# Layer 1 of the tails in seven products, all steady z by DMA transposes, and a reordered head

## The chip, the cores and the metric

The kernel runs on one core of a Trainium2 chip. The metric is the device time of one execution in microseconds (us); lower is better. A core has TensorE (matmuls, into the eight PSUM banks), VectorE (DVE), ScalarE (ACT), GpSimd (POOL) and SyncE (SP), which here only issues DMAs. Each engine runs its instructions in the order of the program and waits for others by semaphores.

## What is computed

Windowed causal attention over 8 images of 8 heads, 576 positions and 64 features, then a normalised two-layer perceptron with a residual. Cut to what matters:

```
scores = (q @ k.T) / 8          # keys i-63 .. i only
attn   = exp(scores) / sum      # per row
x      = attn @ v               # heads side by side: 512 features
z      = (x - mean) / sqrt(var + 1e-6)
out    = x + relu((z * g) @ W1) @ W2    # W1: 512 x 2048, W2: 2048 x 512
```

## The kernel before

**Tiling.** The work is cut into nine groups of 512 tokens: the first 512 positions of each of the eight images (groups 0 to 7), and the 64 last positions of all eight ("tails", group 8). A group has four blocks of 128 tokens. For a block, `s_mm` makes the scores on TensorE and their exponentials on ScalarE, `s_mask` masks them on VectorE, `b_step` multiplies with v on TensorE and then normalises and takes the statistics on VectorE, `r_step` makes the reciprocal deviation on ScalarE, `z_step` makes z on VectorE, and z is transposed into `zT`, features on partitions, which layer 1 reads. There are two ways for that: `zt_step` (lines 447 to 458), four TensorE transposes into a PSUM tile "tp" and a copy by ScalarE, and `x_step` (lines 460 to 464), one DMA transpose issued by SyncE.

**The order.** The order is written out by hand. Period g runs the perceptron of group g as a list of units, and after each unit a slot of steps for the attention of group g+1, placed by `at(unit, step, ...)`. A steady period (g = 2 to 7) has 16 layer 1 units `l1(hc)`, each four matmuls of 512 columns evacuated by a ScalarE relu into `hrT` (lines 508 to 516), and 14 layer 2 units. Layer 2 uses a seven-product scheme: `presum` makes sums of quarters of `hrT` on VectorE (`sw`), `t_weights` sums of quarters of W2 (`tw`), `product(n, t)` (lines 573 to 596) runs eight matmuls of 256 columns, and `post` (lines 600 to 618) adds a finished product to the output on VectorE, which frees its PSUM bank ("X", "Y" or "Z"). In period 7 the attention of group 8 runs beside. Period 8 has only the perceptron of the tails.

**Steady attention.** For groups 3 to 7, `steps` (lines 781 to 793) places block bj: `b_step` at unit ub (4, 8, 12, 17), `r_step` and `z_step` two and two or three units later, then `x_step` at ub+3 for blocks 0 to 2; block 3 goes by `zt_step` at unit 23. In the same period SyncE issues the loads of the next image but one (`load_qk`, `load_v`), and `x_main` (lines 277 to 286), two DMA transposes for each half of q and k after ScalarE's casts `cast_q`, at units 17 and 19. The first scores of an image follow after unit 0 of the next period. Group 2 is prepared in period 1 with `zt_step` for all four blocks; group 8 in period 7 with `zt_step` at units 3, 7, 12 and 17 (the table `TAILS`, lines 751 to 761).

**The head.** Before period 0 (lines 667 to 724) image 0 is loaded and cast, GpSimd casts q and k (`cast_q`) and v, `t_main` transposes q and k on TensorE, `vB_cur` and `vB_prev` make a copy of v that is shifted by half a block. `w1_cast(i, c, engine, lo, hi)` scales and casts a 512-column piece of W1, piece i = 2*quarter + half of the rows, row chunk c. `keep_clock(n)` runs n matmuls whose result is not used. Casts of image 1, of W2 and later loads are in `rest_of_loads` (lines 731 to 746).

**Buffers.** Pool tags are shared: "pt" (six) for the exponentials, "qk32_x" and "qk16_x" (two each) for loaded and cast q and k, PSUM tags "sc" (2), "xps" (1, two banks), "tp" (2), "mm" (2). `pace(t)` copies one column on GpSimd so that its queue waits for t.

Of the kernel before, what the change touches and what calls it, by code (L numbers as in the profile page):

```python
# [18 lines left out]
def kernel(  # L19
# [129 lines left out]
    def cast_q(b, x, half, act=False):  # L149
        t = qk32.pop((b, x, half))  # L150
        dst = p_in.tile([128, 8, 2, D], FP16, tag=f"qk16_{x}", name=f"qk16_{x}_{b}_{half}")
        qk16[(b, x, half)] = dst
        j = 8 if b < NPE else 2 if x == 1 else 4
        cp(act, dst[:, :].rearrange("p (a j) e d -> p a e j d", j=j),
           t[:, :].rearrange("p (a e j d) -> p a e j d", e=2, j=j, d=D))

    def alloc_v(b):
        vA[b] = p_va.tile([128, 4, H, D + 1], FP16, tag="vA", name=f"vA_{b}")
        nc.gpsimd.memset(vA[b][:, :, :, D:D + 1], 1.0)
# [18 lines left out]
    def cast_v(b, c0, c1, act=False):  # L178
        cp(act, vA[b][:, c0:c1, :, 0:D], v32[b][:, c0:c1])
# [72 lines left out]
    def alloc_qkT(b):  # L252
        qkT[b] = [p_qkt.tile([128, NHP, SM + 64 * x], FP16, tag=f"qkT{x}", name=f"qkT{x}_{b}") for x in range(2)]
        if b >= NPE:
            nc.gpsimd.memset(k_runs(b)[:, :, 0:32], 0.0)
        else:
            nc.gpsimd.memset(qkT[b][1][:, :, 0:64], 0.0)
# [4 lines left out]
    def evac(x, out, in_):  # L262
        if x == 0:
            nc.scalar.copy(out=out, in_=in_)
        else:
            nc.vector.tensor_copy(out=out, in_=in_)

# [98 lines left out]
        ptv = pt[:, :].rearrange("p a h w i -> p (a h w) i")  # L366
        nc.vector.tensor_tensor(out=ptv, in0=ptv, in1=mb, op=ALU.mult)  # L367

    def b_step(g, kb):
        kblk = f"{g}_{kb}"  # L370
        if kb % 2 == 0:
            x_norm[(g, kb // 2)] = p_xn.tile([128, 2, H, D], FP32, tag="xn", name=f"xn_{kblk}")
        xn = x_norm[(g, kb // 2)][:, kb % 2]
        xps = ps_x.tile([128, H, 128], FP32, tag="xps", name=f"xps_{kblk}")
        pt = pts.pop((g, kb))
        for h in (0, 2, 4, 6, 1, 3, 5, 7):
            par, hp = h % 2, h // 2
            for r in range(2):
                if g == NGRP - 1:
                    rhs = vt8[:, kb, r, h, :]  # L380
                else:
                    rhs = (vA if r else vB)[g][:, kb, h, :]
                nc.tensor.matmul(out=xps[64 * r:64 * r + 64, h, :D + 1], lhsT=pt[:, par, hp, r, :], rhs=rhs,  # L383
                                 start=True, stop=True)
        rcp = p_blk.tile([128, H], FP32, tag="rcp", name=f"rcp_{kblk}")
        rcps[(g, kb)] = rcp
        nc.vector.reciprocal(out=rcp, in_=xps[:, :, D])
        rcp_b = bass.AP(tensor=rcp.tensor, offset=rcp[:, :].offset,
                        ap=[rcp[:, :].ap[0], rcp[:, :].ap[1], [0, D]])
        nc.vector.tensor_tensor(out=xn, in0=xps[:, :, 0:D], in1=rcp_b, op=ALU.mult)  # L390
        stats = p_blk.tile([128, nc.vector.BN_STATS_DIM], FP32, tag="stats", name=f"stats_{kblk}")
        nc.vector.bn_stats(out=stats, in_=xn.rearrange("p h d -> p (h d)"))  # L392
        mv = p_blk.tile([128, 2], FP32, tag="mv", name=f"mv_{kblk}", bufs=5)
        nc.vector.bn_aggr(out=mv, in_=stats)
        mvs[(g, kb)] = mv
# [97 lines left out]
    def presum(g, i, c):  # L493
        hr = hrTs[g]
        A = [[hr[:, 8 * d + 4 * c:8 * d + 4 * c + 4, 256 * a:256 * a + 256] for d in range(2)] for a in range(2)]
        if c == 0:
            sw[i] = p_hrt.tile([128, 8, 256], FP16, tag=f"sw{i}", name=f"sw{i}_{g}")
        S = {n: t[:, 4 * c:4 * c + 4] for n, t in sw.items()}
        a, b, op = {1: (A[1][0], A[1][1], ALU.add), 2: (S.get(1), A[0][0], ALU.subtract),
                    3: (A[0][0], A[1][0], ALU.subtract), 4: (A[0][1], S.get(2), ALU.subtract)}[i]  # L500
        nc.vector.tensor_tensor(out=S[i], in0=a, in1=b, op=op)  # L501

    def mlp_units(g, split=0, two=False):
        hrT = p_hrt.tile([128, NHC, 512], FP16, tag="hrT", name=f"hrT_{g}")
# [121 lines left out]
                        units.append(lambda kb=kb, part=part: l2(kb, part))  # L626
        if g == 1:
            return units
        for hc in range(split, NHC):
            units.append(lambda hc=hc: l1(hc))  # L630
        if two:
# [33 lines left out]
    )  # L665
    nc.vector.tensor_scalar(out=mbias, in0=mask, scalar1=-1.0, scalar2=30000.0, op0=ALU.add, op1=ALU.mult)
    alloc_qkT(0)
    cast_q(0, 0, 0)
    alloc_v(0)
    cast_q(0, 1, 0)  # L670
    init_vB(0)
    cast_v(0, 0, 1)
    cast_v(0, 1, 2)
    cast_qk(0, 1)
    cast_v(0, 2, 3)
    cast_v(0, 3, 4)
    w1_cast(0, 0, nc.gpsimd)
    w1_cast(1, 0, nc.gpsimd, 0, 256)
    w1_cast(1, 0, nc.gpsimd, 256, 512)
    for i, lo in ((2, 0), (3, 0), (2, 256)):  # L680
        w1_cast(i, 0, nc.gpsimd, lo, lo + 256)

    for f in (alloc_qkT, alloc_v, init_vB):
        f(1)

    def keep_clock(n, pool=ps_t, tag="tp"):
        warm = pool.tile([128, 512], FP32, tag=tag, name="warm")
# [6 lines left out]
    keep_clock(9, ps_mm, "mm")  # L694
    t_main(0, 0, 0, 0)
    keep_clock(1, ps_mm, "mm")
    t_main(0, 1, 0, 1)
    keep_clock(1, ps_mm, "mm")
    vB_cur(0, 0, 0)
    vB_cur(0, 1, 0)  # L700
    vB_prev(0, 0, 1)
    vB_prev(0, 1, 1)
    s_mm(0, 0, True)
    s_mm(0, 1, True, (ps_mm, "mm"))
# [8 lines left out]
    vB_cur(0, 2, 0)  # L713
    keep_clock(2, ps_mm, "mm")
    s_mm(0, 2, True)
    vB_cur(0, 3, 1)
    vB_prev(0, 2, 1)
    keep_clock(1)
    zt_step(0, 1)
    w1_cast(0, 1, nc.scalar)  # L720
    b_step(0, 2)
    z_step(0, 2)
    w1_cast(1, 1, nc.scalar)
    s_mm(0, 3, True)


    load_qk(1, 0)
    for i in range(4):
        w2_load(i)

    def rest_of_loads():
        cast_qk(1, 0)
        for i in range(8):
            w2_cast(i)
            if i < 4:
                w2_load(i + 4)
        load_v(1, 0, 2)
        cast_v(1, 0, 1)
        cast_v(1, 1, 2)
        load_qk(1, 1)  # L740
        load_v(1, 2, 4)
        cast_qk(1, 1)
        cast_v(1, 2, 3)
        cast_v(1, 3, 4)
        load_qk(2, 0)
        load_qk(2, 1)

    def tail_casts(i, act, *us):
# [7 lines left out]
            *tail_casts(3, True, 22, 27, 27), (23, x_tail, 3), (23, x_prev, 3), (24, b_step, 8, 0),  # L756
            (24, s_mm, 8, 1)),
        7: ((0, s_mask, 8, 1), (0, z_step, 8, 0), (3, s_mask, 8, 2), (1, b_step, 8, 1), (1, s_mm, 8, 2),
            (3, zt_step, 8, 0), (8, s_mask, 8, 3), (6, b_step, 8, 2), (6, s_mm, 8, 3), (7, zt_step, 8, 1),
            (11, b_step, 8, 3), (12, zt_step, 8, 2), (17, zt_step, 8, 3)),  # L760
    }
    for g in range(NGRP):
        units = mlp_units(g, (8, 16)[g] if g < 2 else 0, g == 0)
# [17 lines left out]
        def steps(bg, bj, ub, us, sg, sj):  # L781
            if us is not None:
                score(us, bg, bj)
            late = ub < 15
            at(ub, b_step, bg, bj)
            if sj < 4:
                score(ub, sg, sj)
            at(ub + 2, r_step, bg, bj)
            at(ub + 2 + (not late), z_step, bg, bj)
            if bj < 3:  # L790
                at(ub + 3, x_step, bg, bj)
            else:
                at(23, zt_step, bg, bj)

        b = g + 1
        if g == 0:
            at(0, b_step, 0, 3)
            at(0, z_step, 0, 3)
            at(0, w1_cast, 2, 1, nc.scalar)
            at(0, w1_cast, 3, 1, nc.scalar)  # L800
            at(0, w1_cast, 3, 0, nc.scalar, 256, 512)
            at(1, zt_step, 0, 2)
            at(2, zt_step, 0, 3)
            for j in range(4):
# [24 lines left out]
            at(26, keep_k, 0)  # L829
            at(27, lambda: nc.gpsimd.memset(vt8[:, :, :, :, D:D + 1], 1.0))  # L830
            at(27, keep_v, 0)
            at(28, alloc_qkT, 2)
            at(28, cast_q, 2, 0, 0)
            at(29, cast_q, 2, 1, 0)
            at(29, make_vB_half, 1)
            at(41, lambda: pace(zT[1][:, 0, 0:1]))
            at(41, cast_q, 2, 0, 1)
            at(43, cast_q, 2, 1, 1)
        if g == 1:
# [27 lines left out]
            for j in range(4):  # L867
                at((13, 16, 19, 22)[j], s_mm, 2, j)
                at((14, 17, 20, 23)[j], s_mask, 2, j)
                bz((16, 19, 22, 25)[j], 2, j)  # L870
                at((20, 23, 26, 29)[j], zt_step, 2, j)
        if g > 0:
            if g == 1:
                for u, i, c in ((12, 1, 0), (13, 1, 1), (14, 2, 0), (15, 2, 1)):
                    at(u, t_weights, i, c)
            if g == 2:
                at(9, late_masks, 8)
                for u, i, c in ((2, 3, 0), (3, 3, 1), (8, 4, 0), (24, 4, 1)):
                    at(u, t_weights, i, c)
            for u, i, c in () if g == 1 else (  # L880
                    (5, 3, 0), (9, 3, 1), (13, 1, 0), (13, 2, 0), (16, 1, 1), (16, 2, 1), (20, 4, 0), (22, 4, 1)):
                at(u, presum, g, i, c)
        if g > 1 and b < B:
# [21 lines left out]
        if 0 < g and b + 1 < B:  # L905
# [5 lines left out]
            if g == 1:  # L911
# [7 lines left out]
                at(12, alloc_v, n)  # L919
                at(12, alloc_vB, n)  # L920
                for u, c, j in ((21, 0, 0), (22, 1, 0), (24, 2, 1), (24, 3, 1)):
                    if c < 3:
                        at(u, (lambda j=j: pace(zT[b][:, 0, 128 * j:128 * j + 1])) if c % 2 == 0 else
                           (lambda j=j: pace(rss[(b, j)])))
                    at(u, cast_v, n, c, c + 1)
                at(24, make_vB, n)
                at(26, keep_v, n)
            else:
# [4 lines left out]
                for u, x, half in ((16, 0, 0), (16, 1, 0), (17, 0, 1), (18, 1, 1)):  # L933
                    at(u, cast_q, n, x, half, True)
                at(17, x_main, n, 0)
                at(19, x_main, n, 1)
                for c in range(4):
                    at((18, 20, 20, 21)[c], cast_v, n, c, c + 1, True)
                at(22, make_vB, n)
# [38 lines left out]
```

## Time and profile before

| what | us |
|---|---|
| runs shown: median (lowest, highest) | 303.54 (303.21, 303.9) |
| profiled execution | 304.84 |
| its span on the core | 303.0 |
| TensorE busy | 289.7 |
| VectorE, ScalarE, GpSimd busy | 194.8, 189.9, 108.8 |
| periods: 2, 3, 4, 5, 6 start at | 92.6, 122.4, 152.2, 182.0, 211.7 |
| period 7, then 8, start at | 242.7, 271.7 |
| last TensorE instruction ends | 297.8 |

The span is the time from the first to the last instruction of the program in one profiled execution; the rest of the execution lies around it. All lines of the profile belong to that execution. In a row for a group of instructions the numbers after the bar are busy time in us and the mean of one in ns, then the idle time of the engine before them and what ended it. L512 is line 512 of the kernel. PE is TensorE, PEld its weight loads, SPq SyncE's issues.

### The profile page before, as it was taken

Reading aid. Unit: us, or ns where it says so; the run is one execution under the profiler, and the core shown is the slowest. Engines: PE = TensorE matmul, PEld = TensorE weight load, DVE = VectorE, ACT = ScalarE, POOL = GpSimd, SP = SyncE. Lnnn points to the kernel's source line nnn. Section 1 sums busy time; section 2 is a strip of 40 time slices with the busy share of each in tenths; the row PEclk is TensorE's granted clock in tenths of the full one; section 3 lists DMA queues with packets and bytes.
Section 4 is the critical chain, followed back from the end, with each engine's and each line's share of the span. In section 5 each row is a group of like instructions: output and inputs, shape, how many; then the busy total and the mean of one; then the engine's idle time right before and its main releaser. Section 6 shows DMA issues by size and latency. Waiting matters only on the chain.

```text
span 303.0 us, 7956 instructions
## 1 busy us (share of the span) xinstructions
PE 289.7 (96%) x3259; PEld 187.1 (62%) x3259; DVE 194.8 (64%) x353; ACT 189.9 (63%) x372; POOL 108.8 (36%) x194
## 2 busy tenths in 40 slices
PE   5788999999999999999999999999999999999993
PEld 2456544765854478547855784578457845884582
DVE  0696317457984997389638954895489877641362
ACT  3598733576856894589368937892785978307500
POOL 3778775997786203400440043004171010000000
PEclk9799999999999999999999999999999999999999
DMA  6999799999957969997999899899967930003005
GB/s 186 279 368 386 252 272 276 278 303 279 219 115 209 259 127 168 298 247 128 189 319 228 105 200 322 196 118 204 276 123 153 158 141 0 2 21 117 2 0 138
DMA packets 108371, 58.03 MB, mean 192 GB/s; under 512 B 82240, under 2 KB 98112, under 8 KB 108336
## 3 DMA queue, kind: packets, MB, share of 16 engines
q1 hardware_dynamic: 103696, 45.50, 67.1%
q0 software_dynamic: 3680, 11.52, 12.6%
q10 hardware_dynamic: 960, 0.53, 0.6%
q8 instruction: 25, 0.41, 0.6%
q14 instruction: 10, 0.08, 0.1%
HBM read 36.70 MB, written 9.44 MB: 152 GB/s over the span
## 4 chain that ended last, share of the span: by engine, by line
PE 75%; DMA 11%; SPq 5%; POOL 3%; ACT 2%; DVE 2%; issue 1%; POOLq 0%
PE hps L512 33%; PE wX L590 16%; PE wZ L590 8%; PE wY L590 4%; DMA v<-in_v_dram 4%; PE xps L383 4%; SPq L83 3%; DMA w2s<-in_moe_w_ch_dram 3%; PE sc L326 2%; PE ch L525 2%; DMA vt<-vA 2%; SPq L173 2%; PE hph L549 2%; DMA qk<-in_k_dram 1%; PE ztp L453 1%; PE sc L333 1%
## 5 line engine op out<-in xcount | busy, mean ns | idle before, releaser
L512 PE MATMUL hps<-zT,w1g 128*128 128x512 f16 x480 | 109.7, 379 | 0.0
L516 ACT ACTIVATE hrT<-hps 128x512 f16<-128x512 f32 x120 | 71.3, 596 | 54.0 <-PE hps L512 52.8
L512 PEld LDWEIGHTS <-w1g 128*128 128x128 f16 x480 | 44.8, 98 | 49.5
L590 PEld LDWEIGHTS <-sw 128*128 128x128 f16 x448 | 43.5, 98 | 5.0
L590 PEld LDWEIGHTS <-hrT 128*128 128x128 f16 x336 | 32.4, 98 | 5.4
L367 DVE TENSOR_TENSOR pt<-pt,mask 128x1024 f16<-128x1024 f16 x28 | 20.0, 713 | 20.9 <-ACT pt L347 12.6
L207 POOL DMA_DIRECT2D vB<-vA x10 | 5.1, 518 | 77.9 <-ACT vA L145 77.6
L472 POOL DMA_DIRECT2D out_dram<-osb x20 | 13.2, 660 | 54.4 <-DVE osb L608 50.1
L392 DVE BATCH_NORM_STATS2 stats<-xn 128x6 f32<-128x512 f32 x36 | 25.0, 695 | 1.2
L390 DVE TENSOR_TENSOR xn<-xps,rcp 128x512 f32<-128x512 f32 x36 | 24.9, 691 | 1.2
L347 ACT ACTIVATE pt<-sc 128x512 f16<-128x512 f32 x40 | 23.7, 594 | 2.5 <-PE sc L326 2.5
L501 DVE TENSOR_TENSOR sw<-hrT 128x1024 f16<-128x1024 f16 x28 | 19.0, 678 | 9.7 <-ACT hrT L516 9.7
L549 PE MATMUL hph<-zT,w1g 128*128 128x256 f16 x192 | 23.7, 273 | 0.4 <-POOL w1g L240 0.2
L414 DVE TENSOR_SCALAR z<-xn,mv,rs 128x512 f16<-128x512 f32 x32 | 19.8, 617 | 5.0 <-ACT rs L404 4.5
L608 DVE TENSOR_TENSOR osb<-wX,xn 128x512 f32<-128x512 f32 (+1 forms) x24 | 14.9, 621 | 9.9 <-PE wX L590 9.9
L353 ACT ACTIVATE pt<-sc 128x512 f16<-128x512 f32 x32 | 17.6, 594 | 5.0 <-PE sc L333 4.6
L147 POOL CAST qk<-qk 128x1024 f16<-128x1024 f32 x16 | 17.1, 1076 | 9.0 <-DMA qk<-in_q_dram 6.0
L549 PEld LDWEIGHTS <-w1g 128*128 128x128 f16 x192 | 17.9, 98 | 3.5 <-POOL w1g L240 0.5
L383 PEld LDWEIGHTS <-pt 128*64 128x64 f16 x576 | 12.1, 110 | 12.8 <-issue 8.5
L525 PE MATMUL ch<-w2s,hrT 128*128 128x512 f16 x80 | 19.8, 379 | 0.0
L456 ACT COPY zT<-ztp 128x512 f16<-128x512 f16 x21 | 12.3, 584 | 9.6 <-PE ztp L453 9.5
L554 ACT ACTIVATE hrT<-hph 128x512 f16<-128x512 f32 x24 | 14.2, 598 | 3.4 <-PE hph L549 3.2
(108 smaller groups left out, 439.3 us busy)
## 6 DMA issues: line engine op xcount, KB each, us to landing
w2s<-in_moe_w_ch_dram SPq DMA_DIRECT2D x12, 512.0 KB, 9.4
out_dram<-osb POOLq DMA_DIRECT2D x12, 512.0 KB, 7.0
qk<-in_q_dram SPq DMA_DIRECT2D x10, 512.0 KB, 7.7
qk<-in_k_dram SPq DMA_DIRECT2D x10, 512.0 KB, 9.5
v<-in_v_dram SPq DMA_DIRECT2D x40, 128.0 KB, 5.9
qk<-in_q_dram SPq DMA_DIRECT2D x12, 256.0 KB, 5.0
qk<-in_k_dram SPq DMA_DIRECT2D x12, 256.0 KB, 4.8
v<-in_v_dram SPq DMA_DIRECT2D x12, 256.0 KB, 5.7
```

Source lines behind the costliest of these rows:

```text
L347: nc.scalar.activation(out=pt[:, par].rearrange("k h w (p j) -> k (h w) p j", j=4), in_=sc[:, :].rearrange("k h w (j p) -> k (h w) p j", j=4),
L367: nc.vector.tensor_tensor(out=ptv, in0=ptv, in1=mb, op=ALU.mult)
L383: nc.tensor.matmul(out=xps[64 * r:64 * r + 64, h, :D + 1], lhsT=pt[:, par, hp, r, :], rhs=rhs, start=True, stop=True)
L390: nc.vector.tensor_tensor(out=xn, in0=xps[:, :, 0:D], in1=rcp_b, op=ALU.mult)
L392: nc.vector.bn_stats(out=stats, in_=xn.rearrange("p h d -> p (h d)"))
L414: nc.vector.tensor_scalar(out=z, in0=x, scalar1=mv[:, 0:1], scalar2=rss[(g, kb)][:, 0:1], op0=ALU.subtract, op1=ALU.mult)
L501: nc.vector.tensor_tensor(out=S[i], in0=a, in1=b, op=op)
L512: nc.tensor.matmul(out=hps, lhsT=w1g[:, kc, 128 * hc:128 * (hc + 1)], rhs=zT[g][:, kc, :], start=(kc == KCS[0]), stop=(kc == KCS[-1]),)
L516: nc.scalar.activation(out=hrT[:, hc, :], in_=hps, func=AF.Relu, bias=0.0, scale=1.0)
L525: nc.tensor.matmul(out=ch[kb], lhsT=hrT[:, hc, 128 * kb:128 * (kb + 1)], rhs=w2s[:, hc, :], start=(hc == 0), stop=(hc == NHC - 1),)
L549: nc.tensor.matmul(out=hps[:, e], lhsT=w1g[:, kc, 128 * hc:128 * (hc + 1)], rhs=zT[g][:, kc, 256 * half:256 * half + 256], start=(kc == KC ...
L590: nc.tensor.matmul(out=xyz[bank][t * two_banks][:, t], lhsT=lhsT, rhs=rhs, start=bool(first and (t == 0 or two_banks) and hc == 0), stop=( ...
```

## The change

- `steps` uses `x_step` for all four blocks of groups 3 to 7 (block 3 at unit 20 instead of `zt_step` at 23); the second `x_main` moves from unit 19 to 20. Blocks 0 to 2 of group 2 and all blocks of group 8 use `x_step` too.
- Layer 1 of group 8 becomes seven products. `l1_wsum` makes four sums of quarters of W1 on VectorE in eight instructions, `l1_zsum` four sums of quarters of zT, both in period 7. `l1_seven` runs 28 units of four matmuls of 256 columns. Of the seven results for each r, three are copied by ScalarE into SBUF (`held`), one is a ScalarE relu, three are added to a held one on VectorE and then clamped at zero, by VectorE for product 3 and by GpSimd for products 1 and 7. The first layer 2 product goes in before the last four of these units, and the `presum` slots of group 8 move.
- Head: `cast_k0` casts the first half of k on VectorE instead of GpSimd; period 1's memsets move ahead of the first casts; the copies of v change engines, two going to GpSimd; W1 casts go from ScalarE and GpSimd to VectorE, two of them between the normalisation and the statistics of block 2 (`mid`), others change engine or range; six `keep_clock` matmuls are placed around the scores and blocks 1 and 2, where there was one.
- Order: v of image 1 is loaded and cast before the last four pieces of W2; casts of image 2 and the second half of image 1's shifted v go from units 28 and 29 to 39 of period 0, behind z of block 1; two paces of period 1 change.

```diff
+    def cast_k0():
+        t = qk32.pop((0, 1, 0))
+        dst = p_in.tile([128, 8, 2, D], FP16, tag="qk16_1", name="qk16_1_0_0")
+        qk16[(0, 1, 0)] = dst
+        for e in range(2):
+            nc.vector.tensor_copy(out=dst[:, :, e], in_=t[:, 512 * e:512 * e + 512].rearrange("p (j d) -> p j d", d=D))
...
+    def l1_wsum(i, c):
+        A = [[w1g[:, 2 * kb + c, 1024 * d:1024 * d + 1024] for kb in range(2)] for d in range(2)]
+        if c == 0:
+            s1w[i] = p_in.tile([128, 2, 1024], FP16, tag=f"qk32_{i % 2}", name=f"s1w_{i}")
...
+        nc.vector.tensor_tensor(out=S[i], in0=a, in1=b, op=op)
...
+    def l1_zsum(g, i):
...
+        nc.vector.tensor_tensor(out=T[i], in0=z_block(g, *a), in1=b, op=ALU.subtract)
...
+        def product(r, n):
+            kind = {1: "X", 6: "X", 7: "X", 4: "X", 2: "Y", 5: "Z", 3: "Z"}[n]
+            ps, first = bank(r, kind)
+            for e in range(2):
+                hc = 2 * r + e
+                for c in range(2):
...
+                    nc.tensor.matmul(out=ps[:, e], lhsT=lhsT, rhs=rhs, start=bool(first and e == 0 and c == 0),
+                                     stop=(e == 1 and c == 1), skip_group_check=True)
+            up, down = slice(2 * r, 2 * r + 2), slice(8 + 2 * r, 10 + 2 * r)
+            if n in (2, 5, 6):
+                held[(r, n)] = p_pt.tile([128, 2, 256], FP32, tag="pt", name=f"l1h_{r}_{n}")
+                nc.scalar.copy(out=held[(r, n)], in_=ps)
+            elif n == 4:
+                nc.scalar.activation(out=hrT[:, down, lo], in_=ps, func=AF.Relu, bias=0.0, scale=1.0)
+            else:
+                out, other = {1: (hrT[:, up, lo], 2), 7: (hrT[:, down, hi], 5), 3: (hrT[:, up, hi], 6)}[n]
+                nc.vector.tensor_tensor(out=out, in0=ps, in1=held.pop((r, other)), op=ALU.add)
+                (nc.vector if n == 3 else nc.gpsimd).tensor_scalar(out=out, in0=out, scalar1=0.0, scalar2=None,
+                                                                   op0=ALU.max)
+
+        order = ((0, 2), (0, 1), (1, 2), (1, 1), (0, 5), (0, 6), (2, 2), (1, 6), (1, 5), (0, 7), (2, 1), (1, 7),
+                 (3, 2), (3, 1), (0, 3), (0, 4), (2, 5), (2, 6), (3, 5), (3, 6), (1, 3), (2, 7), (1, 4), (3, 7),
+                 (2, 3), (2, 4), (3, 3), (3, 4))
...
+        if last:
+            units += l1_seven(g, hrT)
+            units.insert(24, lambda: product(1, 0))
+            units.append(lambda: product(1, 1))
...
     alloc_qkT(0)
+    alloc_qkT(1)
+    alloc_v(0)
+    alloc_v(1)
     cast_q(0, 0, 0)
-    alloc_v(0)
-    cast_q(0, 1, 0)
     init_vB(0)
+    init_vB(1)
+    cast_k0()
...
+    vB_prev(0, 2, 2)
+    vB_cur(0, 3, 2)
     w1_cast(0, 0, nc.gpsimd)
-    w1_cast(1, 0, nc.gpsimd, 0, 256)
-    w1_cast(1, 0, nc.gpsimd, 256, 512)
-    for i, lo in ((2, 0), (3, 0), (2, 256)):
-        w1_cast(i, 0, nc.gpsimd, lo, lo + 256)
-
-    for f in (alloc_qkT, alloc_v, init_vB):
-        f(1)
+    for i, c, lo in ((1, 0, 256), (1, 1, 256), (2, 0, 0), (2, 0, 256), (3, 0, 256)):
+        w1_cast(i, c, nc.gpsimd, lo, lo + 256)
...
-    vB_cur(0, 3, 1)
-    vB_prev(0, 2, 1)
-    keep_clock(1)
+    w1_cast(0, 1, nc.vector)
+    keep_clock(2, ps_mm, "mm")
     zt_step(0, 1)
-    w1_cast(0, 1, nc.scalar)
-    b_step(0, 2)
+    keep_clock(2, ps_mm, "mm")
+    b_step(0, 2, lambda: [w1_cast(1, c, nc.vector, 0, 256) for c in range(2)])
     z_step(0, 2)
-    w1_cast(1, 1, nc.scalar)
     s_mm(0, 3, True)
+    keep_clock(2, ps_mm, "mm")
...
-            (3, zt_step, 8, 0), (8, s_mask, 8, 3), (6, b_step, 8, 2), (6, s_mm, 8, 3), (7, zt_step, 8, 1),
-            (11, b_step, 8, 3), (12, zt_step, 8, 2), (17, zt_step, 8, 3)),
+            (1, x_step, 8, 0), (8, s_mask, 8, 3), (6, b_step, 8, 2), (6, s_mm, 8, 3), (4, x_step, 8, 1),
+            (11, b_step, 8, 3), (9, x_step, 8, 2), (14, x_step, 8, 3)),
...
-            if bj < 3:
-                at(ub + 3, x_step, bg, bj)
-            else:
-                at(23, zt_step, bg, bj)
+            at(ub + 3, x_step, bg, bj)
...
-            at(0, w1_cast, 3, 1, nc.scalar)
-            at(0, w1_cast, 3, 0, nc.scalar, 256, 512)
+            at(0, w1_cast, 3, 1, nc.scalar, 0, 256)
+            at(0, w1_cast, 3, 0, nc.scalar, 0, 256)
+            at(0, w1_cast, 3, 1, nc.scalar, 256, 512)
...
+            if g == NGRP - 2:
+                for u, i, c in ((14, 3, 0), (15, 3, 1), (17, 1, 0), (18, 1, 1), (20, 2, 0), (22, 2, 1),
+                                (24, 4, 0), (26, 4, 1)):
+                    at(u, l1_wsum, i, c)
+                for u, i in ((24, 1), (26, 2), (28, 3), (28, 4)):
+                    at(u, l1_zsum, g + 1, i)
...
-                at(19, x_main, n, 1)
+                at(20, x_main, n, 1)
```

## The prediction

> **What bounds the kernel now.** I read the page's busy line first, then the chain of waits, then TensorE's own timeline, then SyncE's queue, then rows of single operations.
>
> ```profile
> PE 289.7 (96%) x3259; PEld 187.1 (62%) x3259; DVE 194.8 (64%) x353; ACT 189.9 (63%) x372; POOL 108.8 (36%) x194
> ...
> 271.74 13.81 PE hps L512 x64
> 285.56 1.75 PE wX L590 x16
> ```
>
> The second and third lines are from the chain of waits (start, length, what). A busy TensorE may still wait inside its busy time, so I divide: 64 matmuls of 512 columns in 13.81 us are 216 ns each, 16 of 256 columns in 1.75 us are 109 ns each. From 79 us to 297.8 us the chain is TensorE alone in these steps with nothing between, so there each TensorE instruction removed is time removed. Starts of successive matmuls show no wait over 0.7 us after 28.5 us. After 297.8 us come one DVE add, the output DMAs and the end, 5.2 us that the change leaves alone.
>
> ```profile
> 259.13 1.91 PE L590 MATMUL wX<-w2s,hrT 128*128 128x256 f16 x16
> 260.88 0.39 PE L453 MATMUL ztp<-ident,z 128*128 128x128 f16 x4
> 261.10 1.15 PE L590 MATMUL wY<-w2s,hrT 128*128 128x256 f16 x9
> ```
>
> The timeline of TensorE: a group of four transposes holds back the next matmul by 261.10-260.88 = 0.22 us.
>
> ```profile
> 23.37 0.94 PE L549 MATMUL hph<-zT,w1g 128*128 128x256 f16 x7 [0.24 <-POOL w1g L240]
> 25.41 0.40 PE L453 MATMUL ztp<-ident,z 128*128 128x128 f16 x4 [1.10 <-DVE z L412]
> ```
>
> The last waits of the head are on a W1 cast and on z of block 3; from 25.6 us TensorE is packed. So the head ends where z(0,3) ends.
>
> ```profile
> 136.97 5.00 SPq L464 DMA_TRANSPOSE zT<-z  x3
> 142.06 1.26 SPq L279 DMA_TRANSPOSE qkT<-qk  x1
> 143.42 1.29 SPq L283 DMA_TRANSPOSE qkT<-qk  x1
> 144.80 1.29 SPq L279 DMA_TRANSPOSE qkT<-qk  x1
> 146.19 1.28 SPq L283 DMA_TRANSPOSE qkT<-qk  x1
> 147.52 1.20 SPq L93 DMA_DIRECT2D qk<-in_q_dram  x1
> ```
>
> SyncE's queue in a steady period: one issue follows the other without a gap, and from the loads at 118.23 us to those at 147.52 us it takes 29.3 us of a 29.8 us period. It is the second resource with next to no slack.
>
> ```profile
> L240 POOL TENSOR_SCALAR w1g<-w1s,g 128x512 f16<-128x512 f32 x1 | 1.8, 1755 | 1.3 <-DMA w1s<-in_moe_w_ch_dram 1.3
> L147 POOL CAST vA<-v 128x512 f16<-128x512 f32 x16 | 10.2, 648 | 1.4 <-DMA v<-in_v_dram 1.3
> L608 DVE TENSOR_TENSOR osb<-wX,xn 128x512 f32<-128x512 f32 x18 | 12.4, 687 | 6.8 <-PE wX L590 6.8
> L501 DVE TENSOR_TENSOR sw<-hrT 128x1024 f16<-128x1024 f16 x28 | 19.0, 678 | 9.7 <-ACT hrT L516 9.7
> ```
>
> Groups by form: what GpSimd and VectorE take for forms near the new ones (the second number after the bar is ns of one).
>
> **What the Trainium skill says.** "GPSIMD Engine Reference", section 4.1, calls one-input elementwise work on GpSimd roughly line-rate. This trace agrees for the cast (648 ns for 512) and not for TENSOR_SCALAR (1755 ns for 512, 980 for 256). "SBUF — State Buffer", "Who interferes with whom", says that VectorE copies and tensor_scalars in a two-port mode exclude GpSimd and the other way round: z(0,3) took 1.58 us beside GpSimd's memsets of period 1's buffers, z(0,2) 0.49 us. "DMA: Bandwidth & Descriptors", "DMA Transpose (X-bar)", has plain DMA transposes on SyncE and ScalarE queues only; here all 39 are on SyncE's, so new ones must fit in there.
>
> **The change part by part**, against the profiled execution (span 303.0, with 1.8 us around it 304.84).
>
> *Transposes.* zt_step leaves TensorE 12 times: block 3 of images 3 to 7 (5), blocks 0 to 2 of image 2 (3), the four tail blocks (4). 12 x 0.22 = -2.7 us. The 12 evacuations of 0.58 us on ScalarE go too, worth nothing, since TensorE doesn't wait for ScalarE there. Each new transpose takes 1.25 us of SyncE's issue and lands 3.0 us after it (median of 15; 5.2 at most). Needs: z(3,3) is ready at 116.0, lands by 119 to 121, and layer 1 reads it at 122.2: covered. Behind it, the second half's x_main (moved to unit 20) now waits for z. In the period of 142 us: z ready 145.8, issue to 147.1, the q half issued 147.2 instead of 144.80, landing 3.3 to 4.5 us later, 150.5 to 151.7; scores read it at 152.96-0.22. Covered by 1 us; the k half is 2.4 us later (issue 148.5), but the first two score blocks don't read its keys: at 123.2 scores ran before the last x_main had landed (123.6). In period 1 the q half goes from 85.0 to 88.0 us, lands about 92, is read at 92.7. Loads of the next image follow 2.2 us later. I take +0.2 us; bounds 0 and, where the queue overflows, the rival below. In the tail period SyncE is idle: nothing.
>
> *Layer 1 of the tails.* 64 x 216 ns = 13.8 us become 28 products x 4 x 109 ns = 12.2 us: -1.6 us. The weight loads (98 ns) still hide. Now evacuation: 16 ScalarE (0.6 us), 12 VectorE adds (0.69), four VectorE and eight GpSimd clamps. ScalarE and VectorE fit in 12 us. The GpSimd clamp is a TENSOR_SCALAR of 512 elements, not shown with 16-bit input. Bounds: 0.5 us (below the cast, the narrower input) and 1.9 us (the slowest L240, 1858). I take 1.75, the same operation. Replayed: first product in at 0.9 us, its partner's copy done at 1.3, add to 2.0, first clamp from 2.2; six clamps back to back end at 2.2+6x1.75 = 12.7. The first layer 2 product (unit 24, start 10.5) reads their last rows at 11.1: it waits 1.6 us. The last two clamps end at 16.2, and the presums of VectorE queued behind them make a later product about 0.4 us late. +2.0 us at 1.75; nothing below about 1.5; +3.2 at 1.9. Layer 1 alone would then give back its gain.
>
> *Sums for it in period 7.* Eight l1_wsum (0.68) and four l1_zsum (estimate 0.35, half the elements) put 6.8 us on VectorE, which is busy 19.3 of 29.0 us there; 12 of the 13.9 us after unit 14 would be filled in-order ahead of the adds that free PSUM banks. With 0.61 us from start to start, as two independent ones show (263.05, 263.65 us), the adds come just in time; with 0.72 (dependent ones) replay gives 1.4 us of waits. I take +0.2.
>
> *Head.* VectorE loses the k evacuation (1.23 us) and two vB copies (1.3), gains the cast of k (two of about 0.5), two vB copies of chunks 0 and 1 (1.2), the W1 casts (0.5 and two of about 0.3): even. z(0,2) comes about 0.6 us later because two casts stand before its statistics, z(0,3) about even, but the memsets that stood beside it have moved to the idle time before 4.8 us, which may return up to 1 us. Against it, ScalarE now casts the lower columns of W1 piece 3 for both row chunks (0.5 more) before unit 2, and that read waits already. The clock matmuls run inside waits (216 ns each). GpSimd's v casts before w2 cast 4 delay the last four w2 casts by 1.2 us; layer 2 reads them 1.5 us after they end now. Loads of v 10 us earlier and the later casts of image 2 lie beside packed TensorE work. I take -0.3; bounds -1.0 and +0.8.
>
> Sum: -2.7-1.6+2.0+0.2+0.2-0.3 = -2.2. Against 304.84 that is 302.6; the median of the runs shown is 303.54, 1.3 below the profiled one, and less 2.2 gives 301.3.
>
> **Rivals.** (a) The clamp is cheap, at the cast's speed or below: only the 2.0 us fall away, 299.3. For it, casts at 0.65; against it, both shapes of L240 lie on 0.23 us + 3 ns an element.
> (b) SyncE overflows, slower than before. The steady cycle of 29.3 us gets another 1.35 us: 30.7 against a period of 29.6. It decides once waits inside the cycle (1.0 to 1.8 us for z and casts) no longer absorb it. Then 1.1 us per period over five periods is 5.5, less 1.5 us of slack before scores, so 4 us: 301.3+4 = 305.3. For it, the engines of DMA are 0.99 busy from 123 to 153 us; against it, their share falls to 0.44 at 140 to 142 us, and SyncE waits there for z and casts.
> (c) The head ends later (+0.8) and the VectorE waits of period 7 come (+1.4): 301.3 + (0.8+0.3) + (1.4-0.2) = 303.6, no change. For it, the head's last waits and a VectorE that is two thirds busy in period 7; against it, both need their worst bound.
>
> **How the numbers follow.** Forecast 0.45, (a) 0.17, (b) 0.23, (c) 0.15. No change that can be measured is 0.2% (0.6 us). Faster: 0.43 of the forecast's 0.45, all of (a), a little of (c): 0.61. Same: 0.02 of the forecast's, 0.06 of (c), 0.01 of (b): 0.09. Slower: the rest, 0.30. The forecast's own range is 300.2 to 302.7. The range must reach (a) and most of (b): 299.2 to 305.2.
>
> **What would show it.** TensorE should have 48 fewer L453 transposes and 0.22 us less at each place; layer 1 of the tails spans 12.2 us plus a wait of the first layer 2 product for GpSimd; the clamp's row says 1.75 or less. Waits of score matmuls for a DMA at the start of periods would show (b), L608 ending waits in period 7 (c), the first packed TensorE instant against 25.6 us the head. The prediction is wrong if a wait that I priced at nothing appears in all steady periods, or if the clamp lies far from 1.75.

## The result and the profile after

| kernel | median us (lowest, highest) | runs |
|---|---|---|
| before | 303.49 (303.21, 303.9) | 4 |
| after | 313.42 (312.48, 314.16) | 4 |

The ratio is 1.032, 95% interval 1.029 to 1.036: about 9.9 us slower, where 2.2 us faster was forecast. The profiled execution of after took 312.48 us with a span of 310.6. It is the fastest of its four, while that of before (304.84) was a long one, so the two traces differ by 7.6 us, not by 9.9. Runs more than 1.5% above the fastest of their kernel are left out of the ratios and intervals here and below.

The first part of the page, busy time by engine, and the fourth, the shares of the chain of waits:

```profile
PE 290.5 (94%) x3264; PEld 190.1 (61%) x3264; DVE 209.1 (67%) x385; ACT 182.0 (59%) x358; POOL 121.1 (39%) x203
...
PE 34%; DMA 28%; DVE 12%; SPq 11%; ACT 7%; issue 3%; POOL 3%; ACTq 0%; DVEq 0%; POOLq 0%
PE hps L601 21%; DMA qkT<-qk 12%; DMA w2s<-in_moe_w_ch_dram 6%; DMA v<-in_v_dram 6%; ACT qk L145 4%; PE wX L679 3%; SPq L83 3%; DVE osb L697 3%; SPq L174 3%; DVE sw L512 3%; SPq L180 3%; DMA vt<-vA 2%; SPq L233 2%; DMA zT<-z 2%; DVE z L425 2%
```

TensorE has less to do: 48 transposes fewer, 112 matmuls of 256 columns in place of 64 of 512 in layer 1 of the tails, and five `keep_clock` matmuls more, which makes five instructions more in all. Yet it is busy 0.8 us longer. The chain, which before was TensorE alone from 79 us on, now goes through DMAs: transposes of q and k hold 12% of it, 37 of 310.6 us. The view of waits from 92 to 290 us (us in total, times, longest) says who pays:

```profile
POOL kprev L125 <- DMA qkT<-qk: 16.5, 5, 6.6
...
PE sc L335 <- DMA qkT<-qk: 6.7, 5, 2.4
...
PE hps L601 <- DMA zT<-z: 2.6, 2, 2.2
```

Scores wait for transposed q five times, layer 1 for transposed z twice, always at the start of a period. The starts of successive matmuls, less the time of the matmul in between, measure these delays: 1.32 us at 92.75, 2.48 at 124.80, 2.58 at 156.95, 0.90 at 187.42, 2.38 (layer 1) at 218.28, 0.40 at 219.76, 0.50 (layer 1) at 251.69. They sum to 10.6 us. GpSimd's 16.5 us hold up no matmul: none of TensorE's waits in this view is for GpSimd.

One of these places, the start of period 4. Timelines of SyncE, of GpSimd and of TensorE (start, length, what, and in brackets the idle time before):

```profile
147.32 1.19 SPq L475 DMA_TRANSPOSE zT<-z  x1
148.60 1.31 SPq L288 DMA_TRANSPOSE qkT<-qk  x1
150.00 2.37 SPq L292 DMA_TRANSPOSE qkT<-qk  x1
```

```profile
148.08 1.02 POOL L214 DMA_DIRECT2D vB<-vA  x2 [20.48 <-ACT vA L145]
149.10 0.99 POOL L216 DMA_DIRECT2D vB<-vA  x2
150.08 0.98 POOL L134 DMA_DIRECT2D vt<-vA  x2
```

```profile
153.28 1.03 PE L601 MATMUL hps<-zT,w1g 128*128 128x512 f16 x4
154.24 0.32 PE L335 MATMUL sc<-qkT,qkT 64*64 64x64 f16 x16
156.95 0.32 PE L335 MATMUL sc<-qkT,qkT 64*64 64x64 f16 x16 [2.40 <-DMA qkT<-qk]
```

The transpose of the q half (L288) is issued at 148.60 and its landing is recorded at 156.91, 8.3 us later. The scores start at 156.95. From 148.08 to 151.07 us GpSimd issues six copies of v by DMA (`make_vB`, L214 and L216, and `keep_v`, L134). In before the order was the other way round: the q half was issued at 144.80 and landed 3.4 us later, at 148.20, and the copies were issued 1.8 us and more after it:

```profile
146.58 1.03 POOL L207 DMA_DIRECT2D vB<-vA  x2 [20.46 <-ACT vA L145]
147.60 0.50 POOL L209 DMA_DIRECT2D vB<-vA  x1
```

The view of one line's instructions gives the time from issue to landing for the eight q transposes of images 4 to 7 (min/median/max), first before, then after; the first transpose of each image still lands after 3.2 to 3.9 us, the second is the slow one:

```profile
DMA to landing us min/median/max: 3.2/3.3/3.4
```

```profile
DMA to landing us min/median/max: 3.2/5.3/8.3
```

After the longest wait for layer 1 the granted clock (the share of its full clock that TensorE was given) fell too. The table by stretches (length; busy time of PE, PEld, DVE, ACT, POOL; then the clock, the DMA share and GB/s):

```profile
218.00:219.90 1.90, 1.41 (x35) 0.69 (x36) 0.00 (x0) 0.56 (x1) 0.00 (x0) 0.99 1.12 325
219.90:223.30 3.40, 3.40 (x24) 1.30 (x18) 0.18 (x1) 1.72 (x4) 0.00 (x0) 0.50 1.14 324
223.30:226.00 2.70, 2.70 (x58) 1.41 (x57) 0.79 (x3) 1.79 (x3) 0.39 (x1) 1.00 1.07 163
```

At half clock for 3.4 us TensorE does 1.7 us of work, so 1.7 us more are lost. Waits and clock make 12.3 us. Against them stand gains that the two traces show: 12 x 0.22 = 2.6 us of transposes, 1.0 us in period 8, and a start of period 1 that is 1.4 us earlier, which is a matter of the two executions and not of the change, as the section on the other parts shows. 12.3 - 5.0 = 7.3; the last TensorE instruction ends 7.4 us later.

### The profile page after: what moved, and what is told of

The parts are those of the page before. It is cut to its first block, busy times and chain, and to the rows that moved or that the text cites. A ratio compares the mean times of both kernels' runs of the same rounds, so it can differ in the third digit from the quotient of the medians.

```text
span 310.6 us, 8062 instructions
## 1 busy us (share of the span) xinstructions
PE 290.5 (94%) x3264; PEld 190.1 (61%) x3264; DVE 209.1 (67%) x385; ACT 182.0 (59%) x358; POOL 121.1 (39%) x203
## 4 chain that ended last, share of the span: by engine, by line
PE 34%; DMA 28%; DVE 12%; SPq 11%; ACT 7%; issue 3%; POOL 3%; ACTq 0%; DVEq 0%; POOLq 0%
PE hps L601 21%; DMA qkT<-qk 12%; DMA w2s<-in_moe_w_ch_dram 6%; DMA v<-in_v_dram 6%; ACT qk L145 4%; PE wX L679 3%; SPq L83 3%; DVE osb L697 3%; SPq L174 3%; DVE sw L512 3%; SPq L180 3%; DMA vt<-vA 2%; SPq L233 2%; DMA zT<-z 2%; DVE z L425 2%
## 5 line engine op out<-in xcount | busy, mean ns | idle before, releaser
L601 PE MATMUL hps<-zT,w1g 128*128 128x512 f16 x416 | 96.8, 384 | 2.6 <-DMA zT<-z 2.6
L605 ACT ACTIVATE hrT<-hps 128x512 f16<-128x512 f32 x104 | 61.9, 595 | 49.0 <-PE hps L601 47.4
L601 PEld LDWEIGHTS <-w1g 128*128 128x128 f16 x416 | 38.9, 99 | 47.3 <-issue 5.5
L214 POOL DMA_DIRECT2D vB<-vA x10 | 5.1, 516 | 76.2 <-ACT vA L145 75.9
L638 PEld LDWEIGHTS <-w1g 128*128 128x128 f16 x192 | 17.9, 98 | 4.3 <-DVE w1g L247 1.0
L414 ACT ACTIVATE rs<-mv,epst 128x1 f32<-128x1 f32 x36 | 10.7, 298 | 13.6 <-DVE mv L405 13.6
L396 DVE RECIPROCAL rcp<-xps 128x8 f32<-128x8 f32 x36 | 7.3, 202 | 16.2 <-PE xps L392 16.2
L147 POOL CAST qk<-qk 128x1024 f16<-128x1024 f32 x15 | 15.5, 1040 | 4.4 <-DMA qk<-in_q_dram 3.0
```

Source lines behind the costliest of these rows:

```text
L601: nc.tensor.matmul(out=hps, lhsT=w1g[:, kc, 128 * hc:128 * (hc + 1)], rhs=zT[g][:, kc, :], start=(kc == KCS[0]), stop=(kc == KCS[-1]),)
L605: nc.scalar.activation(out=hrT[:, hc, :], in_=hps, func=AF.Relu, bias=0.0, scale=1.0)
L638: nc.tensor.matmul(out=hps[:, e], lhsT=w1g[:, kc, 128 * hc:128 * (hc + 1)], rhs=zT[g][:, kc, 256 * half:256 * half + 256], start=(kc == KC ...
```

## The experiments

**Theories.** The collision theory: the last transposes of a period (z of block 3, then q and k) now run beside GpSimd's DMA copies of v, where both are slow, and TensorE waits for q. The rival is (b) of the prediction: SyncE's queue is too full, and transposes come late because they are issued late. All ratios are to before, with 95% intervals.

### The steady part undone, and done alone

In after, block 3 of images 3 to 7 back to TensorE:

```diff
-            at(ub + 3, x_step, bg, bj)
+            if bj < 3:
+                at(ub + 3, x_step, bg, bj)
+            else:
+                at(23, zt_step, bg, bj)
...
-                at(20, x_main, n, 1)
+                at(19, x_main, n, 1)
```

> The changed kernel, but block 3 of groups 3 to 7 goes back to TensorE transposes at unit 23 and the second x_main to unit 19. Both theories (collision: the second x_main now runs into GpSimd's copies of v; queue: SyncE has more to issue than a period holds) expect the score waits of periods 3 to 6 to vanish: 313.4 less about 9.4 us of waits and 1.6 us of halved clock, plus 5 x 0.22 us, about 303.5. If the waits stay (over 309), the cause lies before period 2.

Measured: 302.83 us, ratio 0.995 (0.993 to 0.998). The score waits of periods 3 to 6 are gone and q lands after 3.3 to 3.8 us. Two delays are left, 1.03 us at 79.0 in period 1 and 1.30 us (q) at 94.1, after the start of period 2. In the texts below this kernel is e1_old_steady.

The same edit the other way round in before, `x_step` for block 3 and the second `x_main` at unit 20, and nothing else of the change:

> The kernel before with only block 3 of groups 3 to 7 by DMA transpose at unit 20 and the second x_main at unit 20. Both theories: the score waits of about 9 us and the halved clock appear here alone, less 1.1 us of TensorE transposes: 311 to 314. If it stays within 1 us of 303.5, the waits need the shifted head or period 1 too.

Measured: 315.31 us, ratio 1.039 (1.032 to 1.046). The view of waits from 92 to 262 us in its profiled execution, the longest of its four (318.66 us):

```profile
PE sc L326 <- DMA qkT<-qk: 7.7, 4, 2.7
...
PE hps L512 <- DMA zT<-z: 0.5, 1, 0.5
```

The five steady transposes, with the `x_main` that moves behind them, are the loss by themselves. The clock is halved here too, for 3.4 us at the end of each of the three longest waits for q (from 126.0, 160.2 and 225.0 us). The other parts of the change together are a gain of about 1.4 us, by the run before this one.

### Which transfer is slow, and why

In after, the second `x_main` ahead of z of block 3 again (unit 19):

```diff
-                at(20, x_main, n, 1)
+                at(19, x_main, n, 1)
```

> The changed kernel with the second x_main back at unit 19, ahead of block 3's DMA transpose at unit 20. Same work in SyncE's queue in another order. Collision theory: the q half lands in under 4 us, but the transpose of z of block 3 and the k half run into the copies of v, so layer 1 waits at the period's start, about 2 us each: 308 to 313. Queue theory: nothing gained, 312 to 315.

Its four runs took 313.3 to 324.4 us and the profiled one 322.04, too far apart for a ratio. The fastest lies at the edge of the one forecast and inside the other, so the time decides nothing; the trace shows where the wait goes. Timelines of SyncE and TensorE:

```profile
152.45 1.29 SPq L288 DMA_TRANSPOSE qkT<-qk  x1
153.83 1.30 SPq L292 DMA_TRANSPOSE qkT<-qk  x1
155.22 1.23 SPq L475 DMA_TRANSPOSE zT<-z  x1
```

```profile
163.15 1.17 PE L601 MATMUL hps<-zT,w1g 128*128 128x512 f16 x4 [3.26 <-DMA zT<-z]
```

Now q lands in 3.3 to 3.5 us, and z, which is issued last at 155.22, releases layer 1 at 163.15, 7.9 us later. GpSimd issued its copies from 154.53 on. So it is no property of q: what SyncE issues last meets the copies. Changing the order moves the wait and doesn't remove it.

In after, the copies held back on GpSimd until the q half has landed:

```diff
+                at(22, lambda: pace(qkT[n][0][:, 2, 0:1]))
                 at(22, make_vB, n)
```

> The changed kernel, but GpSimd's copies of v (make_vB, keep_v) in periods 2 to 5 wait until the second x_main's q half has landed. Collision theory: that half lands about 3.5 us after its issue instead of 6.6 to 8.3, the score waits go, and the time falls to 301 to 305; the copies come about 4 us later and may make the first b_step wait, up to 1 us per period. Queue theory: the issue times of SyncE are what they were, so the waits stay: 312 to 315.

Measured: 319.86 us, ratio 1.053 (1.046 to 1.059). The q halves land in 3.2 to 4.8 us and the scores' waits for them in the steady periods go. But the copies, issued some 6 us later in the period and now beside the loads of the next image, are late in their turn, and `b_step` waits for them (view of waits, then the landing of L214, which in after was 2.6 to 5.9 us):

```profile
PE xps L392 <- DMA vB<-vA: 9.4, 3, 3.8
```

```profile
DMA to landing us min/median/max: 4.1/6.9/7.6
```

After each of these three waits the clock is halved for 3.4 us, 1.7 us more each time. The expected 301 to 305 us didn't come, but the landings did: with the copies out of the way q lands in time, and the later place that was tried for the copies is no free one either.

In after, the shifted copy of v (`make_vB` of images 3 to 7) made by GpSimd itself. SyncE's issues stay as they are:

```diff
-                nc.gpsimd.dma_start(out=vB[b][j + 32:j + 64, :], in_=vA[b][j:j + 32, :])
+                nc.gpsimd.tensor_copy(out=vB[b][j + 32:j + 64, :], in_=vA[b][j:j + 32, :])
...
-                nc.gpsimd.dma_start(out=vB[b][j:j + 32, 1:4], in_=vA[b][j + 32:j + 64, 0:3])
+                nc.gpsimd.tensor_copy(out=vB[b][j:j + 32, 1:4], in_=vA[b][j + 32:j + 64, 0:3])
```

> The changed kernel, but the shifted copy of v of images 3 to 7 (make_vB) is made by four GpSimd copies of 32 partitions instead of four DMAs. Collision theory: the second x_main's q half lands about 3.4 us after its issue, the waits of the scores and of layer 1 go in periods 1 to 6, and the time falls by 9.4+1.3+1.6 us to 300 to 303, unless the copies [...] come too late for b_step. Queue theory: SyncE issues as much as before, the waits stay, over 310.

Measured: 303.44 us, ratio 0.999 (0.997 to 1.001), 10 us less than after. The groups by form (busy us, mean ns), and the landing of L288:

```profile
L214 POOL COPY vB<-vA 32x2080 f16<-32x2080 f16 x10 | 21.5, 2148 | 64.8 <-ACT vA L145 64.5
...
L216 POOL COPY vB<-vA 32x1560 f16<-32x1560 f16 x10 | 14.9, 1488 | 0.5
```

```profile
DMA to landing us min/median/max: 3.2/3.2/3.5
```

GpSimd works 7.3 us an image, from issue to landing all transposes of q are back at 3.2 to 3.5 us, and of the score waits one of 0.5 us is left. SyncE issues the same transposes in the same order, one behind the other, without a gap from 148.33 to 152.29 us. It issues the q half at 149.64, 4.3 us before the first layer 1 matmul of period 4 (153.95); in after it was 4.7 us. So an issue that is no earlier suffices, the queue isn't the bound, and rival (b)'s mechanism falls. The price is in period 1, where GpSimd is filled: 0.5 us at 64.2, 0.6 at 79.7, 1.5 at 91.8. And layer 1 still waits for z at 244.9, 0.9 us. In the texts below this kernel is e5_vb_pool. This edit also puts the two `keep_v` copies, still DMAs, some 6 us later, so it doesn't tell the share of those from that of `make_vB`.

### GpSimd copies without the new transposes

To see whether the copies by GpSimd are a gain of their own, the last edit in the kernel with the old steady transposes, and the same two lines in before:

> Block 3 by TensorE as in e1_old_steady, and the GpSimd copies of v. Collision theory: e1 less its waits of period 1 (about 2 us), 300 to 302, and about 1 us slower than e5_vb_pool. Queue theory: as e1, 302 to 304, and much faster than e5_vb_pool.

> The kernel before with only the GpSimd copies of v. TensorE waited for none of these DMAs, so both theories expect no change, 303 to 304.5; slower if GpSimd's copies hold up VectorE's sums.

Measured: 303.50 us, ratio 0.999 (0.997 to 1.001), and 305.57 us, ratio 1.006 (1.003 to 1.009). Both miss what the collision theory expected. The first is neither 1 us slower than e5_vb_pool nor, as the queue theory had it, much faster; the two are equal. Its trace has delays of the same kind in period 1 (idle times of TensorE of 0.9 us before 78.8 and 1.3 before 91.0), and in that of e5_vb_pool TensorE still idles 1.4 us for z and q from 123 us on, more than the 1.1 us of five transposes. The second is slower than expected: GpSimd is late in period 1 and a score waits 3.2 us at 104.7. So the copies by GpSimd are no gain by themselves; in these runs they paid only where transposes would meet the DMAs.

### The other parts, one by one

Layer 1 of the tails in seven products, with its sums, alone in before; the new head and order alone in before; both together; and both with the tails' four `x_step`. In these, groups 2 to 7 are transposed as before. For the last, the edit in after is that of e1_old_steady and

```diff
-                if j < 3:
-                    at((19, 22, 25)[j], x_step, 2, j)
-                else:
-                    at(29, zt_step, 2, j)
+                at((20, 23, 26, 29)[j], zt_step, 2, j)
```

with the two paces of period 1 as before.

> The kernel before with only the seven-product layer 1 of the tails and its sums. By the trace of the changed kernel it should take about 1 us off: 1.6 us of matmuls less 0.5 us of waits: 302 to 303.2. If the sums of period 7 cost something that the other changes hid, no gain.

> Before with the new head and order alone (no new transposes, layer 1 as before). From the traces of before and after: first layer 1 matmul 0.6 us earlier, first score of period 0's end 1.1 us earlier, period 1's start 1.4 us earlier, so 1.1 to 1.4 us below before and about 0.8 us slower than the run with head and seven products. Rival (the earlier head is lost again in period 1 or at the last W2 casts): within 0.5 us of before.

> As the run with the old transposes of groups 2 to 7, and the tails' four on TensorE again: the head and seven-product layer 1 alone. If a transpose taken off TensorE is worth its 0.22 us: 4 x 0.22 = 0.9 us slower than that run, 2.1 us below before. If SyncE's transposes in period 7 cost something too, or gain nothing: same time as that run within 0.3 us.

> After with the old transposes for groups 2 to 7 (TensorE for all of group 2 and block 3 of groups 3 to 7, second x_main at unit 19, the old paces of period 1); kept are the head, seven-product layer 1 and the DMA transposes of the tails. Collision theory: all waits for transposed q and z go, those of period 1 too (79.0 us 1.0, 94.1 us 1.3 us in the kernel with old steady transposes alone, less 3 x 0.22 for transposes back on TensorE), so 1.7 us below that kernel: 3.0 us below before, about 301. Rival (the other three parts work against each other or the period 1 waits come from the new head): no better than 302.8 and a wait over 0.8 us left at 79 or 94 us.

| parts | median us | ratio (95%) |
|---|---|---|
| seven products | 303.28 | 0.997 (0.995 to 1.000) |
| head and order | 303.96 | 1.000 (0.998 to 1.002) |
| both | 303.08 | 0.996 (0.994 to 0.997) |
| both, and tails by DMA | 303.19 | 0.996 (0.995 to 0.998) |

Seven products gain about 0.8 us. The head gains nothing that can be measured: its runs have the time of the rival, though not its reason, since no earlier head was there to be lost. The traces explain why an earlier head was expected. The row of granted clock in 40 slices (7.6 and 7.5 us; digits are tenths of the full clock), first of before, then of the kernel with seven products alone, which has the same head:

```profile
PEclk9799999999999999999999999999999999999999
```

```profile
PEclk9999999999999999999999999999999999999999
```

In before the clock is 0.50 from 8.8 to 12.2 us. The same matmul starts 0.1 us later than in the other trace at 8.6 us and 1.0 us later at 12.4. Then z of block 3 falls beside GpSimd's memsets and takes 1.58 us; in the other trace it is over before they begin and takes 0.49. So period 1 starts at 55.27 us in before and at 54.05 with seven products alone, as early as with the new head (53.88 in after, 54.16 with the head alone). Over all traces it starts at 53.9 to 56.3 us with the old head (four) and at 53.5 to 58.1 with the new one (ten).

The tails' transposes by DMA shorten period 7 from 29.05 to 28.29 us in the traces (4 x 0.22 = 0.88 were due), but in that run's last product VectorE frees a bank later (0.63 instead of 0.28 us of delay at 289.6), and the runs show no gain: 0.9 us was expected, and the intervals of the two kernels overlap. Of the 3.0 us expected from the last kernel, 1.1 came. The waits of e1_old_steady at 79.0 and 94.1 us are gone from its trace as expected, but its runs are no faster than those of that kernel (ratio 0.995, from another set of runs); why that is stays open. The trace of that kernel was one of its longest executions (303.57 us), so its waits need not stand in all.

### A version without the collision

In after, group 2 by TensorE again, and the shifted copy of v by GpSimd only for images 4 to 7 (`NPE` is 3), since GpSimd has no time in period 1, with the two paces of period 1 as before (of the edit one line of two for v is shown):

```diff
-                nc.gpsimd.dma_start(out=vB[b][j + 32:j + 64, :], in_=vA[b][j:j + 32, :])
+                (nc.gpsimd.dma_start if b == NPE else nc.gpsimd.tensor_copy)(out=vB[b][j + 32:j + 64, :], in_=vA[b][j:j + 32, :])
```

> After with group 2's transposes on TensorE again, and the shifted copy of v made by GpSimd copies for images 4 to 7 (image 3 keeps its DMAs, since GpSimd is filled in period 1). Collision theory: no wait for transposed q over 0.5 us from period 4 on, the run takes all of the gain of 5 x 0.22 = 1.1 us over the one with old transposes, less what image 3 still pays (up to 2.5 us at 125 us) and 0.9 us at 245 us: 300.5 to 302.5. Rival (SyncE's queue is the bound once the copies are gone): waits of scores of over 1 us in periods 4 to 7 though landings are 3.3 us, 303 or more.

Measured: 301.97 us (300.94 to 305.17, 11 runs), ratio 0.992 (0.989 to 0.994): faster than before by 2.5 us and than after by 11 to 12 us. It is 1.2 us faster than the last kernel of the table (303.19), which differs only in the five steady transposes, the second `x_main` and these copies, and was measured beside it; 5 x 0.22 = 1.1 us were expected. Timelines of GpSimd and TensorE at the start of period 4:

```profile
148.77 4.36 POOL L214 COPY vB<-vA 32x2080 f16<-32x2080 f16 x2 [17.36 <-ACT vA L145]
153.19 3.00 POOL L216 COPY vB<-vA 32x1560 f16<-32x1560 f16 x2
```

```profile
154.19 1.03 PE L601 MATMUL hps<-zT,w1g 128*128 128x512 f16 x4
155.15 0.45 PE L335 MATMUL sc<-qkT,qkT 64*64 64x64 f16 x32
155.53 0.82 PE L601 MATMUL hps<-zT,w1g 128*128 128x512 f16 x3
```

The scores of 32 matmuls now run through without a wait. Periods 2 to 5 last 29.57 us each, against 29.79 in before: the 0.22 us per transpose that the prediction had. A delay of 0.50 us for layer 1 is left at 244.7, where z of image 7 lands late. The profiled execution (305.17 us) is the slowest of the eleven; in it TensorE waits 2.25 us until 46.98 for a GpSimd cast of W2, which is late there, and the clock is halved from 47.1 to 50.5 us.

## Why the prediction was wrong

**The step that failed** is the landing of the second `x_main`, in its words "landing 3.3 to 4.5 us later, 150.5 to 151.7", "Covered by 1 us", for which it took +0.2 us. It mis-sized the landing. The issue itself moved as worked out (2.4 us later; measured 148.60 against 144.80, less the 2.5 us that scores had lost at 124.80, plus the 1.0 us by which period 3 had begun earlier: 2.3). But the landing took 6.6 to 8.3 us in the four steady periods. The transpose of z of block 3, "covered" with 5.2 us at most, landed 7.3 us after its issue at 210.85 and held layer 1 back by 2.4 us. In place of +0.2 stand 10.6 us of waits, 1.3 of them for the q half issued in period 1 (it landed 5.6 us after its issue), and 1.7 us of lowered clock.

The evidence lay in the trace of before. The view of L283, the k transposes, has

```profile
DMA to landing us min/median/max: 3.1/3.6/6.7
```

The second k half of the period of 142 us is issued at 146.19, just as the copies start at 146.58, and lands at 152.71, 6.5 us later; in the four steady periods it took 4.8 to 6.7 us. The prediction mentions such a late landing (123.6) and takes it only to show that k isn't needed early. A move of 2.4 us put q where k had been. The prediction took the landings of the transposes that run ahead of the copies, and never asked what else moves data at the new time.

**Rival (b)** had the place (scores at the start of periods) and the side, but not the mechanism nor the price: 4 us from SyncE's issues, where 10 to 12 us came from landings with SyncE's queue as it was. Its sign, scores that wait for a DMA at the start of periods, came too: that sign can't tell a late issue from a slow landing.

**Transposes off TensorE**, -2.7: held at each steady place (29.79 to 29.57 us a period). In the tails' period it was 0.76 of 0.88 us, in the runs nothing measurable.

**Layer 1 of the tails**, -1.6: held. From 279.99 us to the first pure layer 2 product at 293.30, less the 1.08 us of the one that stands inside, are 12.2 us.

**The clamp**, +2.0: too high. Groups by form:

```profile
L584 POOL TENSOR_SCALAR hrT<-hrT 128x512 f16<-128x512 f16 x8 | 11.7, 1488 | 0.6 <-DVE hrT L583 0.6
```

At 1.49 us, not 1.75, a weight load of layer 2 waits 0.3 us for it. This is the "nothing below about 1.5" of the prediction's own sum. Rival (a) had the consequence but not the reason: the clamp isn't at the 0.65 us of the cast. With a bank that comes free 0.3 us late near the end, period 8 gained 1.0 us of the 1.6.

**Sums in period 7**, +0.2: nothing; with seven products alone period 7 lasts 29.05 us, as in before. **The head**, -0.3: nothing measurable. The 1.58 us of z(0,3) that it hoped to shorten belonged to that execution. The 0.49 us of z(0,2), set against it, were also beside a GpSimd instruction, a TENSOR_SCALAR from 21.04 to 22.07 us: it was the memsets that cost time there, not any work of GpSimd.

Without the collision the sum comes near, in part by luck. The version above, which has all of the change but three of the transposes, and GpSimd copies besides, is 2.5 us faster than before, where -2.2 was forecast for the whole. Its traces give 9 x 0.22 = 2.0 us for the transposes and 1.0 for period 8, less 0.5 of wait at 244.7. A clamp priced too high and a head that gave nothing offset three transposes fewer and that wait. What stays open: why transposes and copies slow each other, how much of it is due to `keep_v`, and why the runs show no gain from the tails' transposes.

## What to carry to other kernels

Before moving a transfer, list the others whose transfer times overlap the new place, on all queues, and take its landing from an instance that already runs beside them, not from the median. When two transfers disturb each other and neither has a free place, reordering only moves the wait (q, then z, then the shifted v); doing one of them on an engine with idle time removed it here. Count with more than the wait itself: eight of the eleven waits of TensorE over 2 us here came with 1.7 us of lowered clock (next section). And compare the start of a kernel over several runs, since one trace's head can be off by more than the gain sought.

## What the runs showed of the hardware

DMA transposes of half a q issued 0.5 to 1.5 us after the start of GpSimd's DMA copies within SBUF landed 6.6 to 8.3 us after issue in the steady periods, instead of 3.2 to 3.9; those of half a k issued 0.4 to 0.7 us before or 0.1 us after that start landed after 4.8 to 6.7 us (before).

After 20 us, TensorE stood still for over 2 us eleven times in the traces of after, of the steady part alone, of the copies held back, of the GpSimd copies in before and of the last version. With eight of these waits (2.2 to 3.8 us) went a stretch of 3.4 us at half the granted clock, which began between 0.1 us before and 1.6 us after the end of the wait; with three (2.3, 2.4 and 3.0 us) none did. No such stretch lies elsewhere in these traces between 20 us and the last matmul. Whether the wait is the cause wasn't tried.

GpSimd took 1.49 us to clamp 512 elements per partition in place with 16-bit input and output, and 2.15 us to copy 32x2080 elements. VectorE's z of 128x512 took 1.58 us beside GpSimd's memsets and 0.49 us when it was over before them.
